# RWKV attention and cosine router: splitting dense TensorE stages around single groups of transposes

## Chip, cores and metric

The kernel runs on one core of a Trainium2 chip. The metric is the device time of one execution in microseconds (us), the median over runs. TensorE is PE (its weight loads PEld), VectorE DVE, ScalarE ACT, GpSimd POOL, and SyncE, which issues most DMAs, SP.

## What is computed

A linear attention over 768 steps for 4 batches and 8 heads of dimension 48 gives 3072 rows of 384. A router picks one of 8 experts for each row by cosine similarity, and that expert's two layers (384 to 1024 to 384) give the row of the output.

```python
for t in range(S):
    cur = einsum('bhd,bhe->bhde', u * k[t], v[t])
    y[:, :, t] = einsum('bhd,bhde->bhe', r[t], state + cur)
    state = w * state + einsum('bhd,bhe->bhde', k[t], v[t])
x = rows of y, heads side by side                     # 3072 x 384
logits = normalised(x) @ normalised(expert_emb).T / tau
e = argmax(logits); gate = softmax(logits)[e]
out = gate * (relu(x @ w1[e]) @ w2[e])
```

## The kernel before

The attention works in 12 turns (TURNS). Turn t takes chunk t // 2 of 128 steps for two of the four batches; u = 0, 1 numbers these two. Within a turn the chunk falls into two halves of 64 steps (s), and the 8 heads into four pairs (p) of two (par), each head padded to 64 partitions.

What a turn does for the inputs of step t, by function and line:

- `scale_r`, `scale_k` (L377, L373, POOL) multiply R and K by powers of the decay, giving Rw and Kw, a turn ahead.
- `turn_in` (L393, PE) transposes Rw or Kw of one u: four 128x128 transposes into one bank. For u=0 the banks are ps0 (Rw) and ps1 (Kw), for u=1 ps2 and ps3. `take_in` (L409 for Rw, L407 for Kw, ACT) copies the bank to RT or KT, and `own_r` (L420, DVE) writes the second half of RT from the same bank, times u.
- `scores` (L433, PE) multiplies KT and RT of one u into ps0 and ps1 (u=0) or ps2 and ps3 (u=1), in 48x64 tiles, four at a time. `mask` (L448) and `own_terms` (L455), both DVE, read these banks into AT.
- `outer` (L469, PE) multiplies Kw and V into the banks pu0 (first half of the chunk) and pu1 (second half), in 64x64 tiles, for both u. `half_state` (L485; L483 in the first chunk) adds pu0 to the state, `next_state` (L490) adds pu1, both DVE; `decay_state` (L496, POOL) follows.

And a turn later, for its output:

- `with_v` (L524, PE, two phases) and `with_state` (L543, PE, one part for each s) accumulate y in the banks py0 and py1; `between` (L512, ACT) peeks at the banks between the phases; `take_y` (L550, ACT, twice) copies them to YT.
- `turn_y` (L558, PE) transposes YT of u=0 into pu0 and of u=1 into pu1, four transposes each; `take_x` (L562, ACT) copies a bank to X, `keep_x` (L587, SP) stores X in DRAM, `squares` (L593, ACT) sums its squares.
- The router's steps for a chunk (`logits` L600, `take_logits` L608, `choose_a` L639 on POOL, `choose`, `scale` L665, `ranks` L686, `rows_of` L844, `put` L867 and others) are spread over the following turns.

The order on every engine is written by hand. `attention` gives each call a planned time (`plan.at`), turns being PERIOD = 9.4 apart, and `Plan.emit` issues the calls sorted by these times. Each engine runs its instructions in the order in which they were issued; semaphores wait for data and for banks to come free. A number in `plan.at` therefore sets only a place in the queues. `after` makes loads and early weight loads wait for the last PE instruction issued before them.

Before the change, the place of the transposes is set by

```python
plan.at(before + 3.3 + 2.35 * u + 0.47 * place, turn_in, k, t, u, which)
plan.at(at + 4.75, outer, k, t)
plan.at(at + 5.6, half_state, k, t)
plan.at(nxt + a[5] + 0.45 * u, turn_y, k, t, u)
```

so that, in a middle turn, PE does: scores (both u), router matmuls, with_v, with_state (both s), Rw and Kw of u=0, with_v, outer (both u), Rw and Kw of u=1, output of u=0 and of u=1, and in every other turn logits. After turn 11 come the experts (`first_layer` L1165, `group` L1243, `layer2` L1383 and others), which the change doesn't touch.

Of the kernel before, what the change touches and what calls it, by code (L numbers as in the profile page):

```python
# [70 lines left out]
def halves(s):  # L71
    return slice(s * HC, (s + 1) * HC)
# [272 lines left out]
def of(ring, t):  # L345
    return ring[t % len(ring)]
# [111 lines left out]
    )  # L458


def outer(k, t):
    Kw, V = of(k.Kw, t), of(k.V, t)
    last = t // 2 == NCH - 1
    for u in range(2):
        for p in range(NP):
            for s in range(1 if last else 2):
                for par in range(2):
                    h, col = 2 * p + par, (u * NP + p) * D
                    k.last = k.nc.tensor.matmul(  # L469
                        k.U[s][par * DP : (par + 1) * DP, col : col + D],  # L470
                        Kw[halves(s), u, h, :], V[halves(s), u, h, 0:D],
                        start=True, stop=True, skip_group_check=True,
                    )
# [407 lines left out]
def attention(k):  # L881

    plan = Plan()
    P = PERIOD
    end = (TURNS - 1) * P
    for t in range(TURNS):
        at = t * P
        c, bp = divmod(t, 2)
        before, nxt = at - P, at + P
        for i in range(6 if t else 0):  # L890
            when = at - 3 * P + 0.5 + 1.55 * i
            if t < 4:

                if t < 3 and i > 3:
                    continue
                plan.at(when, load, k, t, i // 2 if t > 2 else i % 2, i % 2 if t > 2 else i // 2, slice(0, H), False)
                if t < 3 and i == 3:
                    for v in ((0,), (1, 2))[t - 1]:
                        for w in range(2):
                            plan.at(when + 0.1 * v + 0.01, load, k, v, 2, w, slice(0, H), False)  # L900
                continue
            for j in range(2):
                plan.at(when + 0.75 * j, load, k, t, i // 2, i % 2, slice(j * NP, (j + 1) * NP))
        for u in range(2):
            for which in range(2):

                place = which if t else 1 - which
                if t:
                    plan.at(before + 1.0 + 2 * u + place, scale_k if which else scale_r, k, t, u)
                plan.at(before + 3.3 + 2.35 * u + 0.47 * place, turn_in, k, t, u, which)  # L910
                plan.at(before + 3.8 + 2.4 * u + 0.6 * place, take_in, k, t, u, which)
            plan.at(before + (4.0 if t else 4.75) + 2.6 * u, own_r, k, t, u)
            plan.at(at + 0.9 * u, scores, k, t, u)
            for par in range(2):
                plan.at(at + 0.9 + 1.5 * u + 0.36 * par, mask, k, t, u, par)
                plan.at(at + 1.65 + 1.5 * u + 0.4 * par, own_terms, k, t, u, par)
        if t < TURNS - 1:
            plan.at(at + 4.75, outer, k, t)
            plan.at(at + 5.6, half_state, k, t)
        else:  # L920
            plan.at(at + 5.0, outer, k, t)
            plan.at(at + 5.3, half_state, k, t)
        if c < NCH - 1:
            plan.at(at + 6.2, next_state, k, t)
            plan.at(at + 6.8, decay_state, k, t)
        if t < TURNS - 2:
            a = (1.8, 2.3, 3.3, 4.25, 5.0, 6.65, 7.4, 8.4)
            plan.at(nxt + a[0], with_v, k, t, 0)
            plan.at(nxt + a[1], with_state, k, t)
            plan.at(nxt + a[2], between, k, t)  # L930
            plan.at(nxt + a[3], with_v, k, t, 1)
            for par in range(2):
                plan.at(nxt + a[4] + 0.6 * par, take_y, k, t, par)
            for u in range(2):
                plan.at(nxt + a[5] + 0.45 * u, turn_y, k, t, u)
                plan.at(nxt + a[6] + 0.5 * u, take_x, k, t, u)
                plan.at(nxt + a[6] + 0.1 + 0.5 * u, keep_x, k, t, u)
                plan.at(nxt + a[7] + 0.7 * u, squares, k, t, u)
        else:

            for when, fn, *args in (
                (
                    (3.0, with_v, 0), (3.5, with_state), (4.6, between), (5.6, with_v, 1),
                    (5.65, take_y, 0), (5.7, take_y, 1), (7.6, turn_y, 0), (7.75, take_x, 0), (7.9, turn_y, 1),
                    (7.76, keep_x, 0), (8.5, take_x, 1), (8.51, keep_x, 1), (9.5, squares, 0), (9.55, squares, 1),
                ),
                (
                    (6.8, with_v, 0), (6.82, with_state, (0,)), (7.5, with_state, (1,)), (7.7, between),
                    (7.8, with_v, 1), (8.2, take_y, 0), (8.4, take_y, 1), (10.0, turn_y, 0), (10.02, turn_y, 1),
                    (10.4, take_x, 0), (10.41, keep_x, 0), (10.5, take_x, 1), (10.51, keep_x, 1),  # L950
                    (10.7, squares, 0), (10.75, squares, 1),
                ),
            )[t - TURNS + 2]:
                plan.at(end + when, fn, k, t, *args)
        if bp == 1 and c < NCH - 1:
            plan.at(nxt + 7.6, logits, k, c)
            plan.at(nxt + 8.6, take_logits, k, c)
            then = nxt + P
            plan.at(then + 1.78, turn_logits, k, c)
            if c < NCH - 2:  # L960
                plan.at(then + 2.42, keep_logits, k, c)
                plan.at(then + 6.9, choose_a, k, c)
                plan.at(then + 7.5, choose, k, c)
                plan.at(then + 8.9, scale, k, c)
                plan.at(then + 9.0, exps, k, c)
                then += P
                plan.at(then + 1.79, ranks, k, c)
                plan.at(then + 2.42, placed, k, c)
                plan.at(then + 7.5, places, k, c)
                plan.at(then + 8.7, gate, k, c)  # L970
                plan.at(then + 8.8, values, k, c)
                plan.at(then + 8.9, rows_of, k, c)
                plan.at(then + P + 3.25, put, k, c)
                plan.at(then + P + 3.95, collect, k, c)
            if c == SETTLE[0]:
                plan.at(then + 2.43, count, k, c)
                plan.at(then + 5.0, settle, k, c)
                plan.at(then + 5.05, settled, k)

    c = NCH - 2  # L980
    for t, fn, *args in (
        (1.0, choose_a, k, c),
        (3.96, first_lists, k, 0),
        (4.0, keep_logits, k, c),
        (4.2, choose, k, c),
        (5.5, scale, k, c),
        (6.3, exps, k, c),
        (6.85, ranks, k, c),
        (6.9, placed, k, c),
        (6.95, count, k, c),  # L990
        (7.3, places, k, c),
        (7.4, settle, k, c),
        (7.45, sort_embeddings, k),
        (7.5, sort_counts, k),
        (8.4, gate, k, c),
        (8.8, values, k, c),
        (8.9, rows_of, k, c),
        (11.2, put, k, c),
        (11.25, collect, k, c),
        (11.3, first_lists, k, 1),  # L1000
        (11.35, settled, k),
    ):
        plan.at(end + t, fn, *args)
# [3 lines left out]
    c = NCH - 1  # L1007
# [790 lines left out]
def kernel(  # L1798
# [43 lines left out]
    with tc.manual_schedule(), ExitStack() as long_ctx:  # L1842
        n.long = long_ctx.enter_context(tc.tile_pool(name="long", bufs=1))
        with ExitStack() as attention_ctx:
            n.aconst = attention_ctx.enter_context(tc.tile_pool(name="aconst", bufs=1))
            rings(n)
            build_first(n)
            n.rt = attention_ctx.enter_context(tc.tile_pool(name="rt", bufs=2))
            attention(n)
        with ExitStack() as experts_ctx:  # L1850
            n.gp1 = experts_ctx.enter_context(tc.tile_pool(name="gp1", bufs=1))
            n.gp = experts_ctx.enter_context(tc.tile_pool(name="gp", bufs=4))
            experts(n)
# [29 lines left out]
```

## Time and profile before

| | |
|---|---|
| Median of 3 runs | 391.32 us (389.54 to 393.18) |
| The profiled execution | 415.55 us, span 413.7 us |
| Mean granted TensorE clock | 0.964 |
| PE busy | 383.0 us, 93% of the span |
| PEld busy | 349.9 us, 85% |
| DVE busy | 236.4 us, 57% |
| ACT busy | 138.2 us, 33% |
| POOL busy | 189.2 us, 46% |
| Chain of waits that ended last | PE 76%, issue 9% |

The attention fills about 8 to 121 us of the span. In the profile, a row of the timeline is start and length in us, engine, line, operation, what is written and read, shapes and number of records; in brackets stands idle time of the engine just before, with what ended it. A matmul of 32-bit floats leaves two records, a transpose one. Lengths of PE rows include the pipeline's latency, so neighbouring rows overlap; starts are measured. In the chain of waits, "issue" is time in which the engine waited for nothing that the profile shows.

### The profile page before, as it was taken

How to read it: one execution, taken by the hardware profiler on the slowest of the kernel's cores; microseconds unless marked ns; L12 is line 12 of the kernel's file. 1: busy time of each engine (PE TensorE's matmuls, PEld its weight loads, DVE VectorE, ACT ScalarE, POOL GpSimd, SP SyncE). 2: the span in 40 equal slices, each digit the busy share in tenths (PEclk: the TensorE clock that was granted, in tenths of full speed). 3: DMA queues.
4: the chain of work that ended last, by engine and by line, in shares of the span. 5: the costliest groups of instructions: out<-in, count | busy, mean ns of one | idle time of the engine just before them, and what ended most of it. 6: DMA issues, size and time to landing. Idle time of an engine off the chain costs nothing.

```text
span 413.7 us, 12753 instructions
## 1 busy us (share of the span) xinstructions
PE 383.0 (93%) x5055; PEld 349.9 (85%) x5055; DVE 236.4 (57%) x603; ACT 138.2 (33%) x357; POOL 189.2 (46%) x222
## 2 busy tenths in 40 slices
PE   8889899999989996999989997699999999999993
PEld 5778788888878895989779997699999989989982
DVE  7957787878885650532843744155546546465331
ACT  4464546465524521221023212221321321422410
POOL 3875656555530354420377427501753855702002
PEclk9999999999996996899999999689999999999998
DMA  9988788788154573263953553144454446101001
GB/s 157 198 165 174 158 172 181 146 183 179 44 178 142 162 238 104 73 164 93 315 178 90 126 182 93 42 111 136 132 137 142 144 133 199 62 10 57 0 2 65
DMA packets 100232, 54.44 MB, mean 132 GB/s; under 512 B 80897, under 2 KB 95275, under 8 KB 100162
## 3 DMA queue, kind: packets, MB, share of 16 engines
q1 hardware_dynamic: 93218, 43.68, 41.6%
q0 software_dynamic: 4448, 9.45, 7.5%
q8 instruction: 42, 0.69, 0.7%
q10 hardware_dynamic: 2496, 0.40, 0.5%
q14 instruction: 28, 0.23, 0.2%
HBM read 44.25 MB, written 9.58 MB: 130 GB/s over the span
## 4 chain that ended last, share of the span: by engine, by line
PE 76%; issue 9%; DVE 2%; another core or an unknown queue 2%; POOL 1%; ACT 1%; POOLq 0%; DVEq 0%; ACTq 0%
PE ps L1243 9%; PE ps L1383 8%; PE ps L1165 7%; PE ps L1364 6%; PE pu L1243 5%; PE ps L433 4%; PE ps L393 4%; PE pu L1383 4%; PE py L1243 4%; PE py L1383 3%; PE pu L558 3%; PE py L524 3%; PE py L1165 3%; PE py L543 2%; PE pu L469 2%
## 5 line engine op out<-in xcount | busy, mean ns | idle before, releaser
L1123 POOL DMA_INDIRECT G<-xs,quarters x76 | 83.7, 1101 | 50.5 <-issue 38.8
L1342 POOL DMA_INDIRECT out_dram<-y,goes x27 | 28.3, 1048 | 97.0 <-DVE y L1352 41.3
L1165 PE MATMUL ps<-RT,w 128*128 128x128 f32 x204 | 30.1, 299 | 4.4 <-ACT R L1168 1.9
L1165 PEld LDWEIGHTS ps<-RT,w 128*128 128x128 f32 x204 | 27.3, 210 | 5.9 <-issue 2.3
L377 POOL TENSOR_TENSOR Rw<-R,rpow 128x384 f32<-128x384 f32 x22 | 22.8, 1037 | 14.2 <-PE ps L433 8.0
L1243 PE MATMUL ps<-xTe,w 128*128 128x192 f32 (+3 forms) x132 | 27.0, 339 | 0.0
L433 PE MATMUL ps<-RT,KT 48*64 48x128 f32 x768 | 25.3, 275 | 0.2
L433 PEld LDWEIGHTS ps<-RT,KT 48*64 48x64 f32 x768 | 21.1, 132 | 3.7 <-issue 2.5
L373 POOL TENSOR_TENSOR Kw<-K,kpow 128x384 f32<-128x384 f32 x22 | 23.8, 1081 | 0.5 <-DMA R<-in_r_dram 0.5
L1243 PEld LDWEIGHTS ps<-xTe,w 128*128 128x128 f32 x132 | 23.4, 194 | 0.1
L496 POOL TENSOR_TENSOR T<-T,wC 128x384 f32<-128x384 f32 x10 | 8.3, 827 | 27.1 <-DVE T L490 27.1
L448 DVE TENSOR_TENSOR AT<-ps,smask 128x256 f32<-128x256 f32 x48 | 18.6, 414 | 1.2 <-PE ps L433 1.2
L409 ACT COPY RT<-ps 128x512 f32<-128x512 f32 x22 | 12.9, 585 | 18.3 <-PE ps L393 16.9
L455 DVE COPY_PREDICATED AT<-dmask,ps 128x256 f32<-128x256 int32 x48 | 18.5, 441 | 0.0
L1270 ACT ACTIVATE RT<-RT 128x384 f32<-128x384 f32 (+1 forms) x18 | 9.5, 532 | 26.1 <-DVE RT L1182 18.6
L1243 PE MATMUL ps<-Tx,S 128*128 128x192 f32 (+3 forms) x76 | 16.5, 348 | 1.2 <-issue 1.1
L420 DVE TENSOR_TENSOR RT<-ps,uw 128x512 f32<-128x512 f32 x22 | 15.2, 690 | 4.2 <-ACT RT L409 3.9
L393 PE MATMUL ps<-ident,Rw 128*128 128x128 f32 x96 | 15.4, 283 | 2.2 <-DVE AT L455 1.0
L1383 PE MATMUL ps<-T,RT 128*128 128x192 f32 x96 | 17.3, 327 | 0.0
L1270 ACT ACTIVATE hT<-hT 128x432 f32<-128x432 f32 (+2 forms) x18 | 9.7, 541 | 21.2 <-DVE hT L1182 16.1
L1383 PEld LDWEIGHTS ps<-T,RT 128*128 128x128 f32 x96 | 15.9, 190 | 0.9
L469 PE MATMUL pu<-V,Kw 64*64 64x48 f32 x704 | 14.4, 218 | 2.4 <-issue 2.3
(380 smaller groups left out, 917.0 us busy)
## 6 DMA issues: line engine op xcount, KB each, us to landing
w<-in_moe_w_dram SPq DMA_DIRECT2D x96, 128.0 KB
w<-in_moe_w_dram SPq DMA_DIRECT2D x24, 384.0 KB
xs<-X SPq DMA_DIRECT2D x24, 192.0 KB
K<-in_k_dram SPq DMA_DIRECT2D x32, 96.0 KB
R<-in_r_dram SPq DMA_DIRECT2D x32, 96.0 KB
V<-in_v_dram SPq DMA_DIRECT2D x32, 96.0 KB
w<-in_moe_w_dram SPq DMA_DIRECT2D x16, 192.0 KB
V<-in_v_dram SPq DMA_DIRECT2D x8, 192.0 KB
```

Of the source, the lines that this page charges most:

```text
L373: q.tensor_mul(of(k.Kw, t)[:, u, :, 0:D], of(k.K, t)[:, u] if t else raw(k, 0)[:, u, :, 0:D], k.kpow)
L377: ins = k.nc.gpsimd.tensor_mul(of(k.Rw, t)[:, u, :, 0:D], of(k.R, t)[:, u], k.rpow)
L393: k.last = k.nc.tensor.transpose(bank[:, p * C : (p + 1) * C], pair(src[:, u], p), k.ident)
L433: ins = k.nc.tensor.matmul(k.D[2 * u + par][halves(s), p * C : (p + 1) * C], KT[rows, u, p, halves(s)], RT[rows, u, p, s].rearrange("q j i ...
L469: k.last = k.nc.tensor.matmul(k.U[s][par * DP : (par + 1) * DP, col : col + D], Kw[halves(s), u, h, :], V[halves(s), u, h, 0:D], start=Tru ...
L1123: k.nc.gpsimd.indirect_dma_start(out=k.GG[e % 2][:, g * QUARTER : (g + 1) * QUARTER], out_offset=None, in_=k.xs.rearrange("n (q c) -> (n q ...
L1165: k.last = k.nc.tensor.matmul(ps, w1[:, m, f * 128 : (f + 1) * 128], x_of(k, e, m)[:, cols], start=(m == 0), stop=(m == NK - 1))
L1243: k.last = nc.tensor.matmul(ps[:, i * h : (i + 1) * h], a[:, g, i * 128 : (i + 1) * 128], b, start=start and i == 0, stop=True, skip_group ...
L1270: nc.scalar.activation(out(i, c), out(i, c), ACT.Relu)
L1342: k.nc.gpsimd.indirect_dma_start(out=out[:, :], out_offset=IndirectOffsetOnAxis(ap=k.goes[0:n, e, t : t + 1], axis=0), in_=y[0:n, :], in_o ...
L1364: k.last = k.nc.tensor.matmul(k.two[e][m], a, b, start=(f == 0), stop=(f == NF - 1))
L1383: k.last = nc.tensor.matmul(ps, a(q), b[:, q], start=start and q == 0, stop=True, skip_group_check=True,)
```

## The change

Four kinds of calls get other planned times; no computation is added or removed.

- `outer` takes its u as an argument and is planned twice, so that `turn_in` of Rw for u=1 can stand between its two parts, and Kw for u=1 after the second. `half_state` moves from at + 5.6 to at + 6.16, just behind `own_r` of u=1, which moves from before + 6.6 to before + 6.15.
- `with_state` is planned for s=0 and s=1 apart, with Rw of u=0 between them and Kw of u=0 after them. In the first chunk, where with_state has no part s=0, Rw of u=0 stands ahead of it.
- `turn_y`, `take_x`, `keep_x` and `squares` of u=1 move to the next turn, where `turn_y` stands between scores of u=0 and of u=1.
- `choose_a` for chunk NCH - 2 moves from 1.0 to 2.3 within the last turn.

```diff
-def outer(k, t):
+def outer(k, t, us=(0, 1)):
...
-    for u in range(2):
+    for u in us:
...
-                plan.at(before + 3.3 + 2.35 * u + 0.47 * place, turn_in, k, t, u, which)
-                plan.at(before + 3.8 + 2.4 * u + 0.6 * place, take_in, k, t, u, which)
-            plan.at(before + (4.0 if t else 4.75) + 2.6 * u, own_r, k, t, u)
+                if t:
+                    plan.at(before + ((2.75, 3.8), (5.3, 6.35))[u][place], turn_in, k, t, u, which)
+                    plan.at(before + ((3.4, 4.4), (6.1, 6.8))[u][place], take_in, k, t, u, which)
+                else:
+                    plan.at(before + 3.3 + 2.35 * u + 0.47 * place, turn_in, k, t, u, which)
+                    plan.at(before + 3.8 + 2.4 * u + 0.6 * place, take_in, k, t, u, which)
+            plan.at(before + ((4.0, 6.15) if t else (4.75, 7.35))[u], own_r, k, t, u)
...
-            plan.at(at + 4.75, outer, k, t)
-            plan.at(at + 5.6, half_state, k, t)
+            for u in range(2):
+                plan.at(at + 4.75 + u, outer, k, t, (u,))
+            plan.at(at + 6.16, half_state, k, t)
...
-            a = (1.8, 2.3, 3.3, 4.25, 5.0, 6.65, 7.4, 8.4)
+            a = (1.8, 2.3, 3.75, 4.25, 5.0, 6.65, 7.4, 8.4)
             plan.at(nxt + a[0], with_v, k, t, 0)
-            plan.at(nxt + a[1], with_state, k, t)
+            for s in range(2):
+                plan.at(nxt + a[1] + s, with_state, k, t, (s,))
             plan.at(nxt + a[2], between, k, t)
             plan.at(nxt + a[3], with_v, k, t, 1)
...
             for u in range(2):
-                plan.at(nxt + a[5] + 0.45 * u, turn_y, k, t, u)
-                plan.at(nxt + a[6] + 0.5 * u, take_x, k, t, u)
-                plan.at(nxt + a[6] + 0.1 + 0.5 * u, keep_x, k, t, u)
-                plan.at(nxt + a[7] + 0.7 * u, squares, k, t, u)
+                over = u * (P + 0.5 - a[5])
+                plan.at(nxt + a[5] + over, turn_y, k, t, u)
+                plan.at(nxt + a[6] + over, take_x, k, t, u)
+                plan.at(nxt + a[6] + 0.1 + over, keep_x, k, t, u)
+                plan.at(nxt + a[7] + over, squares, k, t, u)
...
-        (1.0, choose_a, k, c),
+        (2.3, choose_a, k, c),
```

## The prediction, made before the changed kernel ran

> **What bounds the kernel now.** I read the stages first: busy time, granted clock and DMA share of the attention (16 to 121 us of the span) and of the rest.
>
> ```profile
> 16.00:121.00 105.00, 98.71 (x3098) 87.77 (x3092) 81.59 (x246) 55.80 (x153) 61.47 (x89) 1.00 0.73 157
> 121.00:414.00 293.00, 271.07 (x1783) 252.86 (x1778) 141.27 (x326) 75.24 (x188) 119.71 (x111) 0.95 0.40 120
> ```
>
> The columns are stretch, length, PE, PEld, DVE, ACT, POOL, clock, DMA share, GB/s. In the attention PE is busy 98.71 of 105 us at full clock (1.00). The chain of waits, read next, agrees: from 30 to 122 us it stays on PE almost throughout, and its other pieces are "issue", two of which are
>
> ```profile
> 72.35 0.95 issue
> 90.02 0.43 issue
> ```
>
> With the others in the attention (0.74 at 20.3, 1.00 at 42.0, 1.08 at 50.7, 0.40 at 68.8, 0.51 at 102.5) they come to 5.1 us. They fall inside runs of equal matmuls, where no semaphore is due. So a turn is a queue of PE stages back to back, and whatever lengthens that queue lengthens the kernel. Then one turn of PE in the timeline (start, length):
>
> ```profile
> 78.31 0.69 PE L524 MATMUL py<-AT,V 64*64 64x64 f32 x32
> 78.83 0.63 PE L543 MATMUL py<-RT,T 48*48 48x64 f32 x32
> 79.28 0.63 PE L543 MATMUL py<-RT,Tmid 48*48 48x64 f32 x32
> 79.83 1.10 PE L867 MATMUL pu<-QV,P 128*128 128x64 f32 x8
> 80.77 0.61 PE L393 MATMUL ps<-ident,Rw 128*128 128x128 f32 x4
> 81.22 0.60 PE L393 MATMUL ps<-ident,Kw 128*128 128x128 f32 x4
> 81.75 0.69 PE L524 MATMUL py<-AT,V 64*64 64x64 f32 x32
> 82.26 1.10 PE L469 MATMUL pu<-V,Kw 64*64 64x48 f32 x64
> 83.29 0.66 PE L393 MATMUL ps<-ident,Rw 128*128 128x128 f32 x4
> 83.78 0.60 PE L393 MATMUL ps<-ident,Kw 128*128 128x128 f32 x4
> 84.22 1.10 PE L558 MATMUL pu<-ident,YT 128*128 128x128 f32 x8
> 85.25 1.98 PE L433 MATMUL ps<-RT,KT 48*64 48x128 f32 x64
> ```
>
> Lengths overlap, so I use start to start. Four transposes between transposes take 0.44 (83.78 to 84.22). As the first after a tiled stage they take 0.49 (83.29 to 83.78), and as the last before one 0.53 (81.22 to 81.75). Thirty-two 64-column records take 0.45 after a tiled stage (78.83 to 79.28), 0.52 after transposes (81.75 to 82.26), 0.55 before a full-array stage (79.28 to 79.83). Entering the full array from tiles costs (0.55-0.45)+(0.49-0.44)=0.15 us, leaving it (0.53-0.44)+(0.52-0.45)=0.16. **One interruption of a tiled stage by transposes costs 0.31 us beside the transposes themselves.**
>
> Last, ACT and DVE at the end of that turn:
>
> ```profile
> 82.51 1.07 ACT L550 COPY YT<-py 128x512 f32<-128x512 f32 x2
> 83.40 0.56 DVE L485 TENSOR_TENSOR Tmid<-T,pu 128x384 f32<-128x384 f32 x1 [0.67 <-PE pu L469]
> 83.98 0.58 ACT L409 COPY RT<-ps 128x512 f32<-128x512 f32 x1 [0.40 <-PE ps L393]
> 84.06 0.56 DVE L490 TENSOR_TENSOR T<-Tmid,pu 128x384 f32<-128x384 f32 x1
> 84.60 0.69 DVE L420 TENSOR_TENSOR RT<-ps,uw 128x512 f32<-128x512 f32 x1
> ```
>
> half_state (L485) runs first and frees bank pu0 before the output's transposes need it; own_r (L420) comes last and starts 0.04 after ACT's L409 ends (84.56). The list of waits has the same pair, in whose order lies the trouble below:
>
> ```profile
> DVE RT L420 <- ACT RT L409: 3.9, 6, 1.1
> ```
>
> **What the Trainium skill says.** "TensorEngine Tiling", Key Properties: changing the tiling mode drains TensorE. The trace agrees: 0.15 in, 0.16 out. "TensorE: Matmul & The Clock Gate", Part 1: the clock halves after a window of some 3.4 us with too little PE activity; Part 4: transposes don't count as activity in the same way. Here the clock stays at 1.00 although every turn has a run of 16 transposes (83.29 to 85.25 is one), so the trace gives that no support. "Runtime: NRT & Kernel Launch", Instruction fetch mechanics: instructions arrive in blocks of 256 by the engine's own DMA queue. The page's 42 packets and 0.69 MB on one instruction queue fit PE's 10110 records, and I read the "issue" pieces as late blocks.
>
> **The change, part by part.** No work is added or removed. R and K stand for the transposes of Rw and Kw, Y for those of the output, 0 and 1 for the half u.
>
> 1. *Interruptions.* R1 goes inside outer (turns 0 to 10: 11), R0 inside or ahead of with_state (turns 1 to 10: 10; where L867 follows R0 it shares the full array), Y1 inside scores (turns 2 to 11: 10). In each case the order of PE before had these beside other transposes. 31 x 0.31 = +9.6 us. The seam between Y0 and Y1 (a wait, some 0.05) goes: 10 x 0.05 = -0.5.
>
> 2. *Y0 now waits for half_state.* The changed program's DVE order has own_r of u=1 ahead of half_state and next_state in every turn; before, it was behind. Let S be the start of outer (82.26). PE: half of outer 0.47, in 0.10, R1 0.49, out 0.09, other half 0.47+0.07, in 0.10, K1 0.49: Y0 could start at S+2.28. DVE: ACT ends its two L550 copies at S+1.32, whatever R1 does; L409 for R1 queues behind them, to S+1.90; own_r S+1.94 to 2.63; half_state to S+3.15; with the 0.05 seen between L490's end (84.62) and Y1, Y0 starts at S+3.2. Stall 0.92, against none before (S+1.96), in turns 1 to 9. In turn 10 other DVE work already delays half_state, and I count 0.4. Sum +8.7. Late next are scores, which stand behind Y0, and through decay_state and choose_a the router's work on DVE.
>
> 3. *R0 may wait for the masks of u=0.* It moves 0.45 nearer to scores, while masks queue on DVE behind routing (P, L844, takes 1.49 at 77.69). Following the row from S, bank 0 comes free about 0.2 after PE is ready in turns with P and 0.1 in those with choose: 9 turns, +1.0 (bounds 0 and 3).
>
> 4. *Off the path.* ten take_x and squares of u=1 come a turn later on ACT, which sits idle 3.03 us before L512 at 79.95; if that cover went, 1.1 us each would delay R0's copy, not PE. Their ten stores on SP move behind two K loads and hold the K, R and V loads queued after them; these feed scaling a turn ahead, so 0; without the slack up to 1 us a turn. choose_a in turn 11 has POOL's 3.41 idle us before L1113: 0. POOL's scaling starts when scores of u=0 end, which Y1's move advances: 0.
>
> 5. *Given back.* A turn gains about 1.8 us and holds about 580 PE records with weight loads, 2.3 blocks, so each block gets 0.8 us more to arrive. Taking 0.8 off each late block (1.00 to 0.2, 1.08 to 0.3, 0.95 to 0.15, the others to 0) gives -4.4 (bounds -5.1 and 0: a run without the profiler may have no such holes).
>
> Sum: 9.6-0.5+8.7+1.0-4.4 = +14.4 us. The profiled execution took 415.55 (span 413.7), so its like would take 430. The runs have a median of 391.32, 24 below, but their attention does the same PE work, so I add the same: **405.7**.
>
> Bounds: an interruption 0.15 (half hidden) to 0.35, 4.7 to 10.9; the stall 0 to 1.2 each; with the others +5 to about +24.
>
> **Rivals.**
> - *Drains only* (0.17): own_r does not hold up half_state, say because L409 overtakes. For: turns with much DVE work show it idle. Against: L420 follows L409 each time. 9.1+1.0, less 2.5 given back: +7.6, 399.
> - *The clock falls too* (0.15): the end of a turn would have the stall and 0.75 us of drains in some 4 us. For: after three "issue" holes between 122.2 and 124.4 the clock averages 0.67 over 121 to 131. Against: single 1 us holes at 42 and 51 did not do it. Four half-rate windows of 3.4 us lose 1.7 each: +7, 412.
> - *Instruction supply is the bound* (0.05): waits then vanish under it, 391. The profile gives 5.1 us over some 25 blocks, 0.2 each; it decides from 0.8.
> - *Not slower: the clock gains* (0.08): in unprofiled runs clusters of transposes might halve the clock, and separating them prevent it. Each window saved is worth 1.7; from 9 windows it outweighs 14.4; ten give 388.7. Against: not one between 16 and 121 us.
>
> **How the numbers follow.** The forecast has 0.55, with 400 to 410 as its own range. About 1% is what a measurement of this kernel can tell from no change (its runs spread from 389.54 to 393.18). Faster by over 1% is most of the last rival, 0.06; within 1% supply and its rest, 0.06; slower 0.88. The range 397 to 413 takes in drains only and most of the falling clock.
>
> **What would show it.** In the new profile: 469, 433 and 543 split, each split with 0.3 us beyond its transposes (right if 25 to 40 such); Y0 (L558, first four) idle about 0.9 before it, released by DVE's half_state (wrong if Y0 follows K1 within 0.2); "issue" in the attention below 2 us; the stages from turn 11 on unchanged but later by 14 us; the clock at 1.00 up to there. A clock below 1 in the attention, or turns of unchanged length, would make it wrong.

## The result and the profile after

The changed kernel takes 401.44 us (median of 6 runs, 400.06 to 404.63), the kernel before beside it 391.23 us (6 runs, 389.54 to 393.18). The ratio is 1.0264, with an interval of 1.0225 to 1.0303: slower by about 10.2 us, where 14.4 were forecast. Ratios, here and below, leave out the runs that took over 1.5% longer than the fastest of their kernel.

The two profiled executions can't be set against each other as wholes: the one of before (span 413.7 us) has stretches of half clock after the attention, the one of after (span 399.1) has none before its last microseconds. The attention is free of that in both, so I measure it alone, from the first scores (L433) of turn 0 to the first scores of turn 11. The starts in the traces are 8.81 and 115.69 us before, 10.25 and 127.32 after: **106.9 and 117.1 us, a difference of 10.2 us, the same as the timed one.** In this pair the loss is all in the attention.

The attention as one stretch of the kernel after (stretch, length, PE, PEld, DVE, ACT, POOL, clock, DMA share, GB/s):

```profile
16.00:127.50 111.50, 101.63 (x2925) 83.22 (x2929) 81.90 (x231) 58.16 (x149) 59.98 (x87) 1.00 0.66 140
```

The clock stays at 1.00 throughout the attention, as before; PE is idle for 10 us of it instead of 6. What it waits for is told by the list of waits of PE in the attention (us in total, times, longest), which in the kernel before is "issue" for 5.1 us, R0 for the masks (L455) once for 1.0, and three other pieces of 0.4 and less:

```profile
PE ps L393 <- issue: 2.4, 3, 1.0
PE pu L469 <- issue: 2.3, 3, 1.1
PE ps L393 <- DVE AT L455: 1.0, 1, 1.0
PE py L543 <- issue: 0.4, 1, 0.4
```

Of the kernel after:

```profile
PE pu L558 <- ACT KT L407: 3.8, 5, 0.8
PE ps L393 <- DVE AT L455: 1.9, 3, 0.8
PE pu L558 <- DVE Tmid L485: 1.3, 2, 0.8
PE ps L393 <- POOL Rw L377: 1.1, 2, 0.8
PE pu L558 <- DVE over L828: 0.8, 1, 0.8
PE pu L469 <- issue: 0.4, 1, 0.4
```

"issue" has fallen to 0.4 us: the late instruction blocks are gone. That "issue" on PE is a late block shows in a count of PE's matmul and weight load records in order of start: each of the seven pieces in the attention of the kernel before has 193 or 194 records of its block of 256 ahead of it, and so has every piece in the attention of the other traces. In their place stand the wait ahead of Y0 (L558), 5.9 us in eight pieces, and a longer wait ahead of R0 (L393), 3.0 us for banks (L455) and Rw (L377). The end of a turn in the timeline of after shows the first of them:

```profile
91.33 0.66 PE L393 MATMUL ps<-ident,Kw 128*128 128x128 f32 x4
91.44 0.69 DVE L420 TENSOR_TENSOR RT<-ps,uw 128x512 f32<-128x512 f32 x1 [2.57 <-ACT RT L409]
92.02 0.58 ACT L407 COPY KT<-ps 128x512 f32<-128x512 f32 x1 [0.61 <-PE ps L393]
92.05 0.54 DVE L485 TENSOR_TENSOR Tmid<-T,pu 128x384 f32<-128x384 f32 x1
92.74 0.63 PE L558 MATMUL pu<-ident,YT 128*128 128x128 f32 x4 [0.76 <-ACT KT L407]
```

K1 is done, and DVE, after 2.57 us of waiting for ACT's copy of R1 (L409), does own_r (L420, 91.44) and only then half_state (L485, 92.05 to 92.59), and Y0 starts at 92.74. The profile names ACT's L407 as the releaser: it ends at 92.60, within 0.01 us of half_state. Two engines that end together can't be told apart from such a row; the first experiment does it.

**A sum over gaps.** For every run I took the start-to-start gaps of successive PE records in the attention and divided its length in two: "waits", what a clearly long gap (by some 0.1 us or more) exceeds the ordinary pitch, and "rest". Before: 10.3 + 96.6. After: 13.2 + 103.9. So waits grew by 2.9 us and the rest, where the drains of split stages must lie, by 7.3. The line between the two isn't sharp: a long gap at a change of tiling holds a drain too, and the limit for "long" moves some 1 us from one part to the other.

### The profile page after: what moved, and what is told of

Its sections match the earlier page's. It is cut to its first block, busy times and chain, and to the rows that moved or that the text cites. A ratio compares the mean times of both kernels' runs of the same rounds, so it can differ in the third digit from the quotient of the medians.

```text
span 399.1 us, 12727 instructions
## 1 busy us (share of the span) xinstructions
PE 378.0 (95%) x5055; PEld 339.2 (85%) x5055; DVE 239.7 (60%) x603; ACT 142.4 (36%) x357; POOL 189.1 (47%) x222
## 4 chain that ended last, share of the span: by engine, by line
PE 74%; issue 9%; DVE 6%; POOL 4%; DMA 2%; ACT 2%; POOLq 0%; SPq 0%; DVEq 0%; ACTq 0%
PE ps L1252 10%; PE ps L1392 8%; PE ps L1373 6%; PE ps L1174 6%; PE pu L1252 5%; PE ps L393 5%; PE py L1252 4%; PE pu L1392 4%; PE py L1392 3%; PE ps L433 3%; PE py L524 3%; PE pu L558 2%; PE py L1174 2%; PE py L543 2%; DMA R<-in_r_dram 2%
## 5 line engine op out<-in xcount | busy, mean ns | idle before, releaser
L420 DVE TENSOR_TENSOR RT<-ps,uw 128x512 f32<-128x512 f32 x22 | 15.2, 689 | 21.5 <-ACT RT L409 21.5
L377 POOL TENSOR_TENSOR Rw<-R,rpow 128x384 f32<-128x384 f32 x22 | 22.8, 1036 | 11.1 <-ACT rpow L143 6.4
L1174 PE MATMUL ps<-RT,w 128*128 128x128 f32 x204 | 26.2, 278 | 1.4 <-ACT R L1177 0.6
L433 PE MATMUL ps<-RT,KT 48*64 48x128 f32 x768 | 27.1, 277 | 0.2
L1174 PEld LDWEIGHTS ps<-RT,w 128*128 128x128 f32 x204 | 24.2, 192 | 2.0 <-ACT R L1177 0.8
L433 PEld LDWEIGHTS ps<-RT,KT 48*64 48x64 f32 x768 | 20.8, 133 | 5.0 <-issue 4.0
L558 PE MATMUL pu<-ident,YT 128*128 128x128 f32 x96 | 15.3, 283 | 6.1 <-ACT KT L407 3.8
L448 DVE TENSOR_TENSOR AT<-ps,smask 128x256 f32<-128x256 f32 x48 | 18.5, 413 | 1.0 <-PE ps L433 0.9
L409 ACT COPY RT<-ps 128x512 f32<-128x512 f32 x22 | 12.9, 586 | 17.1 <-PE ps L393 14.8
L558 PEld LDWEIGHTS pu<-ident,YT 128*128 128x128 f32 x96 | 10.1, 141 | 10.1 <-ACT KT L407 6.8
L393 PE MATMUL ps<-ident,Rw 128*128 128x128 f32 x96 | 15.5, 284 | 3.4 <-DVE AT L455 1.9
L455 DVE COPY_PREDICATED AT<-dmask,ps 128x256 f32<-128x256 int32 x48 | 18.5, 438 | 0.0
L407 ACT COPY KT<-ps 128x512 f32<-128x512 f32 x22 | 12.9, 586 | 11.2 <-PE ps L393 10.8
```

Of the source, the lines that this page charges most:

```text
L377: ins = k.nc.gpsimd.tensor_mul(of(k.Rw, t)[:, u, :, 0:D], of(k.R, t)[:, u], k.rpow)
L393: k.last = k.nc.tensor.transpose(bank[:, p * C : (p + 1) * C], pair(src[:, u], p), k.ident)
L433: ins = k.nc.tensor.matmul(k.D[2 * u + par][halves(s), p * C : (p + 1) * C], KT[rows, u, p, halves(s)], RT[rows, u, p, s].rearrange("q j i ...
L558: k.last = k.nc.tensor.transpose(k.rows[u][:, g * C : (g + 1) * C], YT[:, u, g % 2, g // 2, :], k.ident)
L1174: k.last = k.nc.tensor.matmul(ps, w1[:, m, f * 128 : (f + 1) * 128], x_of(k, e, m)[:, cols], start=(m == 0), stop=(m == NK - 1))
```

## The experiments

The last pair (one row again, before again) ran beside a before that takes 391.15 us, the others beside ones of 416.86 (the first four) and 414.21 (the next four), where runs spread over 10 us and more. What is slower there lies behind the attention: the kernel after takes 427.65 us there and has the same attention to 0.1 us. Its clock from 130 to 400 us is 0.97 instead of 0.99, which is some 5 of the 26 us; the rest of them stays open. So ratios from there are wide, and the attention's length is the better measure. The expectations in absolute times took a before of 391 us for granted; of them only the differences count.

| kernel | attention | waits | rest | ratio to before beside it | of the medians of all runs |
|---|---|---|---|---|---|
| before | 106.9 | 10.3 | 96.6 | 1 | 1 |
| before, again | 106.2 | 9.9 | 96.3 | 1.0042 [1.0012, 1.0071] | 1.001 |
| after | 117.1 | 13.2 | 103.9 | 1.0264 [1.0225, 1.0303] | 1.026 |
| after, again | 117.1 | 13.4 | 103.7 | 1.0495 [1.0377, 1.0613] | 1.032 |
| outer split only | 112.4 | 12.0 | 100.4 | 0.997 [0.9864, 1.0075] | 1.013 |
| Y1 in scores only | 107.5 | 9.1 | 98.4 | 1.0134 [1.0046, 1.0222] | 1.004 |
| R0 in with_state only | 109.8 | 11.2 | 98.6 | 1.0172 [1.0108, 1.0237] | 1.007 |
| order on DVE only | 119.8 | 23.2 | 96.6 | 1.0439 [1.03, 1.0578] | 1.034 |
| after, own_r behind | 115.2 | 11.5 | 103.7 | none | 1.024 |
| after, own_r behind, R0 and K0 back | 111.0 | 9.4 | 101.7 | 1.0207 [1.0019, 1.0394] | 1.010 |
| one row of transposes | 111.6 | 15.0 | 96.6 | 1.0253 [1.0133, 1.0373] | 1.009 |
| one row, again | 111.0 | 15.4 | 95.6 | 1.0073 [1.0043, 1.0103] | 1.010 |

The kernel before against itself gives 1.0042, so a ratio that near to 1 says nothing, whatever its interval. Several ratios disagree with their profiles: 5.5 us more of attention are 1.3%, above the interval of the outer's split; 0.7 and 3.0 us are 0.2% and 0.7%, below those of Y1 and R0, and one row and after again lie above what their lengths come to as well. These ratios rest on few runs (the outer's split on 2 of its 22, against 8 of 27 of before). The medians of all runs come within 0.4% of what the lengths give, but for after again (1.032, where 10.2 us are 2.5%), and that stays unexplained. So the argument below rests on the lengths.

### after, own_r behind half_state

```diff
-plan.at(before + ((4.0, 6.15) if t else (4.75, 7.35))[u], own_r, k, t, u)
+plan.at(before + ((4.0, 6.6) if t else (4.75, 7.35))[u], own_r, k, t, u)
```

Theory H: half_state behind own_r is what Y0 waits for. Rival L: ACT's copy of K1, as the profile says.

> The changed kernel with one place altered: own_r of u=1 stands behind half_state and next_state on DVE again. Theory H (Y0 waits for half_state, which own_r delays): the idle time before the output's transposes, 6.1 us in the attention of the changed kernel, falls to about 1 us; some 1 us of late instruction blocks comes back; 396 us, between 394.5 and 398. Rival L (Y0 waits for ACT's copy L407, which the list of waits names for 3.8 of the 6.1 us): the DVE order doesn't matter, 400 to 402. Rival D (31 interruptions of 0.31 us are the whole loss): 400 to 402.

In the timeline of this kernel, at the end of the same turn:

```profile
89.47 0.66 PE L393 MATMUL ps<-ident,Kw 128*128 128x128 f32 x4
89.57 0.55 DVE L485 TENSOR_TENSOR Tmid<-T,pu 128x384 f32<-128x384 f32 x1 [2.56 <-PE pu L469]
90.16 0.59 ACT L407 COPY KT<-ps 128x512 f32<-128x512 f32 x1 [0.61 <-PE ps L393]
90.27 0.63 PE L558 MATMUL pu<-ident,YT 128*128 128x128 f32 x4
90.70 0.68 DVE L420 TENSOR_TENSOR RT<-ps,uw 128x512 f32<-128x512 f32 x1
```

Y0 starts at 90.27, when L407 has only begun (it ends at 90.75), and 0.15 after half_state's end: L is refuted, H stands. But the attention shortened by 1.9 us, not by the 5 that the wait was worth. Its list of PE waits says where the rest went:

```profile
PE ps L393 <- DVE AT L455: 5.9, 6, 1.1
...
PE pu L558 <- DVE Tmid L485: 0.3, 2, 0.2
```

Y0's wait fell from 5.9 to 0.5 (with 0.2 for L483), but R0's rose from 3.0 to 6.2 (0.3 of it for Rw). The size of H's forecast was wrong: it took the stall off PE without asking who is next. DVE was just behind, as the timeline shows earlier in the same turn:

```profile
84.04 0.77 DVE L455 COPY_PREDICATED AT<-dmask,ps 128x256 f32<-128x256 int32 x2
...
84.61 0.63 PE L393 MATMUL ps<-ident,Rw 128*128 128x128 f32 x4 [1.04 <-DVE AT L455]
```

In such a turn DVE has the router's L858 (1.19 us from 80.85) and L844 (1.49 from 81.96) ahead of the masks L448 (from 83.37) and L455, and runs without a break up to the mask that frees R0's bank; a PE that comes earlier waits there.

### Each split alone

The three, each in the kernel before:

```diff
-plan.at(at + 4.75, outer, k, t)
-plan.at(at + 5.6, half_state, k, t)
+for u in range(2):
+    plan.at(at + 4.75 + u, outer, k, t, (u,))      # R1 at before + 5.3
+plan.at(at + 5.9, half_state, k, t)
```

> Before, with only outer split around R1 (own_r behind, as before). Theory H: 11 interruptions x 0.31 = 3.4 us, and since half_state now ends with the second half of outer just as Y0 is due, up to 0.25 us a turn for Y0 and Y1, 2.5 more; 1.5 given back by late blocks: 395.5, between 394 and 397. Rival L: 3.4 less 1, 393.5. Rival D: 3.4, 394.6.

```diff
+over = u * (P + 0.5 - a[5])
-plan.at(nxt + a[5] + 0.45 * u, turn_y, k, t, u)
+plan.at(nxt + a[5] + over, turn_y, k, t, u)        # take_x, keep_x, squares likewise; choose_a as in the change
```

> Before, with only the output's transposes of u=1 moved between the scores of the next turn. Theories H and L: 10 x (0.31 - 0.05) = 2.6 us, 0.6 given back: 393.2, between 392 and 394.5. Rival D: the same without giving back, 393.8. If ACT's later copies or the stores on SP mattered: 395 or more.

```diff
-plan.at(nxt + a[1], with_state, k, t)
+for s in range(2):
+    plan.at(nxt + a[1] + s, with_state, k, t, (s,))  # R0 at before + 2.75, K0 at + 3.8; between at + 3.75
```

> Before, with only with_state split around R0. Theories H and L: 10 x 0.31 = 3.1 us, plus waits of R0 for the masks on DVE or for POOL of 1 to 2 us, 1 given back: 394.8, between 393 and 396. Rival D: 394.3 and no idle time before R0.

In the rest of the sum, where drains are, the outer's split costs 100.4 - 96.6 = 3.8 us, Y1's 1.9, R0's 2.0. Together 7.7, against 7.3 for all three in the kernel after: the costs add up. Divided by the number of splits they are not the price of one, because the rest also takes in short waits and leaves out drains that stand in a long gap. That price is read at the seams, start to start, where nothing is awaited. Y1 in scores only:

```profile
85.82 0.60 PE L558 MATMUL pu<-ident,YT 128*128 128x128 f32 x4
86.35 1.10 PE L433 MATMUL ps<-RT,KT 48*64 48x128 f32 x32
87.38 0.66 PE L558 MATMUL pu<-ident,YT 128*128 128x128 f32 x4
87.97 1.10 PE L433 MATMUL ps<-RT,KT 48*64 48x128 f32 x32
89.01 0.41 PE L686 MATMUL pu<-cum_oh,umask 128*128 128x32 f32 x2
```

From Y0 to the router's L686 these are 3.19 us, where the kernel before takes 2.94 (84.22 to 87.16): 0.25 more. Before has a wait of 0.06 between Y0 and Y1 there (the two take 1.03, and 0.97 where nothing is awaited) that is gone, so the interruption is 0.31. R0 in with_state, in the kernel after in a turn where R0 waits for nothing, and below it the same of the kernel before:

```profile
39.92 0.63 PE L543 MATMUL py<-RT,T 48*48 48x64 f32 x32
40.48 0.66 PE L393 MATMUL ps<-ident,Rw 128*128 128x128 f32 x4
41.07 0.66 PE L543 MATMUL py<-RT,Tmid 48*48 48x64 f32 x32
41.66 0.66 PE L393 MATMUL ps<-ident,Kw 128*128 128x128 f32 x4
42.25 0.69 PE L524 MATMUL py<-AT,V 64*64 64x64 f32 x32
...
47.41 0.63 PE L543 MATMUL py<-RT,T 48*48 48x64 f32 x32
...
49.44 0.69 PE L524 MATMUL py<-AT,V 64*64 64x64 f32 x32
```

2.33 us against 2.03: 0.30 for the interruption (and 0.25 where L867 shares the full array: 3.17 from 62.67 us on, against 2.92 from 78.83 before). In the outer's split, first part, R1 and second part take 1.76 us (100.02 to 101.78 after; outer and R1 1.52 before), and K1 behind a tiled stage 0.49 (78.85 to 79.34 in the outer's own kernel) instead of 0.44: 0.29. So the three stages cost nearly the same. The whole lengths (+5.5, +0.7, +3.0, where +4.3, +2 and +3.6 were expected) differ from these by the waits, whose sum is +1.7, -1.2 and +0.9 against before's. In the outer's split late blocks of 4.8 us remain, and half_state, which needs both parts of outer, now ends behind K1, so that Y0 starts 0.42 after K1's last transpose. R0's split has, on its own, the wait for the masks:

```profile
PE ps L393 <- DVE AT L455: 4.5, 7, 1.0
...
PE ps L393 <- POOL Rw L377: 0.7, 1, 0.7
```

5.2 us for banks and Rw, 3.9 more than before's 1.3, where the prediction had 1.0 for this step: without Y0's stall the move costs much more than with it (3.0 in the kernel after). That is what the first experiment ran into.

### The order on DVE alone

The kernel before with nothing changed on PE:

```diff
-plan.at(at + 5.6, half_state, k, t)
+plan.at(at + 6.61, half_state, k, t)
-plan.at(at + 6.2, next_state, k, t)
+plan.at(at + 6.62, next_state, k, t)
```

> The kernel before with nothing split and nothing moved on TensorE: only half_state and next_state are put behind own_r of the second half on VectorE, as in the kernel after. Compared by the attention's length (first scores of turn 0 to first scores of turn 11, 106.9 us in the kernel before) and by the ratio to the kernel before. Theory D (the order on VectorE makes Y0 wait): here K1's transposes follow R1's at once, so the chain eviction of R1's half by ScalarE 0.58, own_r 0.69, half_state 0.54 stands bare ahead of Y0: about 1.6 to 1.8 us for each of 10 turns, 16 to 18, of which up to 5 us of late instruction blocks come back: +11 to +13, ratio 1.028 to 1.034. Theory S (only the splits cost, the order on VectorE is nothing): 0, ratio 1.00.

The attention is 12.9 us longer (11 to 13 were expected; the ratio of 1.0439 lies above the 1.034 of that text, with 1.03 as its lower end): theory D holds, and its sum too. In the timeline:

```profile
102.45 0.60 PE L393 MATMUL ps<-ident,Kw 128*128 128x128 f32 x4
...
103.27 0.69 DVE L420 TENSOR_TENSOR RT<-ps,uw 128x512 f32<-128x512 f32 x1 [1.59 <-ACT RT L409]
103.88 0.55 DVE L485 TENSOR_TENSOR Tmid<-T,pu 128x384 f32<-128x384 f32 x1
...
104.57 1.15 PE L558 MATMUL pu<-ident,YT 128*128 128x128 f32 x8 [1.52 <-DVE Tmid L485]
```

K1, then 1.52 us of nothing on PE: copy, own_r, half_state, one after the other. The chain is the one that the prediction had, only bare, because no second half of outer stands between R1 and K1. Its rest is 96.6, as before's: nothing was split. (Of its waits, 1.8 us are matmuls stretched by half clock, told of at the end.) The list of waits gives the price and what came back for it:

```profile
PE pu L558 <- DVE Tmid L485: 12.1, 8, 1.5
...
PE ps L433 <- issue: 0.3, 1, 0.3
PE pu L469 <- issue: 0.2, 1, 0.2
```

With 1.5 each ahead of Y0 for L483 and L828 it is 15.1 us of stall, and late blocks of 0.5 instead of 5.1. So the blocks come in time when PE waits: this kernel has no drains beyond before's, and the late blocks are gone as they are in after. Drains alone didn't do that: with the outer's split 4.8 us of late blocks remain, with Y1's 4.9.

### after, own_r behind, and R0 and K0 back

```diff
-plan.at(before + ((2.75, 3.8), (5.3, 6.35))[u][place], turn_in, k, t, u, which)
+plan.at(before + ((3.3, 3.77), (5.3, 6.35))[u][place], turn_in, k, t, u, which)
-for s in range(2):
-    plan.at(nxt + a[1] + s, with_state, k, t, (s,))
+plan.at(nxt + a[1], with_state, k, t)
```

with own_r of u=1 at before + 6.6, as in the first experiment.

> The kernel after with two things undone: own_r of the second half stands behind half_state and next_state, and R0 and K0 come one after the other behind an undivided with_state. Left are the outer's split (11) and Y1 between the scores' halves (10). Theory W (what removing the Y0 stall freed in the run with own_r behind went into R0's wait for the masks, 5.9 us there): with R0 later that wait has cover, so 10 splits fewer (3.1) and about 3 to 5 us of waits less: attention 4 to 6 us longer than before's 106.9, ratio 1.010 to 1.016. Theory P (every stall removed comes back in the next place, wherever it is): attention stays about 115, 8 us longer, ratio 1.020 or more.

The attention is 111.0 us, 4.1 longer than before's: theory W. R0's wait for the masks is down from 5.9 to 1.0, Y0's is 0.4, and late blocks are back, 3.4 us of them:

```profile
PE pu L469 <- issue: 2.4, 3, 1.3
PE ps L393 <- DVE AT L455: 1.0, 1, 1.0
```

Waits are at 9.4, below before's 10.3; what is left of the loss is the rest, +5.1: the drains of outer and scores (3.8 and 1.9 alone).

### One row of transposes a turn

The change turned round:

```diff
-plan.at(at + 4.75, outer, k, t)
-plan.at(at + 5.6, half_state, k, t)
+plan.at(at + 3.35, outer, k, t)
+plan.at(at + 4.3, half_state, k, t)                 # next_state at + 4.9
-plan.at(before + 3.3 + 2.35 * u + 0.47 * place, turn_in, k, t, u, which)
+plan.at(before + 5.2 + 0.9 * u + 0.45 * place, turn_in, k, t, u, which)   # t > 0; copies, own_r and L867 with it
```

> The opposite of the change: in the kernel before the outer product moves ahead to stand right behind with_state, and all six groups of transposes of a turn (R0 K0 R1 K1 Y0 Y1) stand in one row behind the second with_v, so TensorE goes from the tiled stages to whole-array transposes and back once a turn instead of twice. half_state and next_state move ahead with the outer product. Theory D+S: 10 interruptions fewer at 0.31 us are -3.1; own_r and half_state are far from each other; late instruction blocks may take back up to 1: attention 104 to 105, ratio 0.992 to 0.996. Rival: four evictions in a row by ScalarE (0.58 each against 0.31 for a group of transposes) make the scores or Y0 wait for their buffers, 0.3 to 0.5 us a turn: nothing gained or +2, ratio 1.000 to 1.005.

> The kernel with one row of transposes a turn once more. In its first run the clock stood at 0.91 in two stretches of 20 us of the attention, and instruction blocks came late for about 7 us. If the clock was the chip's and not the order's, it is 1.00 in the attention here, and the attention is 3 to 4 us shorter than the 111.6 us of the first run, 107.5 to 109, still not shorter than before's 106.9, because the late blocks remain. If the order itself (16 to 24 transposes in a row, and the tiled stages in one stretch) brings the clock down, it is 0.91 again and the length 111 to 112.

> The kernel before beside it on the same chip: attention 106.9 us at clock 1.00, with some 5 us of late instruction blocks, ratio 1.00. If this chip's clock falls in the attention whatever the order, the clock is below 1.00 there in this run too.

This was meant to beat both and doesn't: 111.6 us of attention, and 111.0 when run again, where the kernel before has 106.2 and 1.00 of clock between 20 and 60 us. Neither of my forecasts held, the rival's of +2 included. (A group of four transposes takes 0.44 us, as the prediction has it, not 0.31.) The list of waits of the second run:

```profile
PE pu L469 <- issue: 3.5, 3, 2.4
PE pu L469 <- DVE lg L627: 3.3, 3, 1.1
PE py L524 <- issue: 2.0, 2, 1.7
```

With 0.8 ahead of L393 there are 6.3 us of late blocks, where before beside it has 4.7: with_v, with_state, outer and scores now follow one another without the pause of transposes. Outer, moved ahead, waits 3.3 us for a bank that the router's logits hold until DVE copies them (L627), and 1.5 us are waits for own_r (L420), the kind that the rival had named. And the clock fell: from 22.3 us on, in the stretches' view (same columns as above),

```profile
18.00:22.30 4.30, 1.93 (x119) 1.80 (x112) 1.91 (x6) 0.22 (x2) 4.22 (x17) 1.00 0.94 182
...
24.00:25.00 1.00, 1.00 (x6) 1.00 (x7) 0.11 (x1) 1.00 (x3) 0.81 (x1) 0.50 1.11 215
...
26.00:27.00 1.00, 1.00 (x11) 1.00 (x10) 0.31 (x1) 1.00 (x3) 0.00 (x0) 1.00 0.49 86
```

PE was busy for 1.93 of 4.30 us, behind a late block of 2.4 us, and then ran at half clock for some 3.4 us (0.58 over 22.3 to 24, 0.50 to 26), which costs about 1.7. The rest is 95.6 with this in it, so about 93.9 without: 2.4 below the 96.3 of before beside it, near the 3.1 forecast for ten drains fewer. By this count the drains were saved; a bank, late blocks, own_r and the clock took more than that.

## Why the prediction was right in direction and too high

By its own steps, in us over the attention (start to start, from the gaps of the two traces):

| step | forecast | measured |
|---|---|---|
| 1. interruptions | 9.1 | 7.3 (8.8 at the seams) |
| 2. Y0's stall | 8.7 | 7.4 |
| 3. R0's wait | 1.0 | 1.9 |
| 4. ACT, SP, POOL | 0 | 0 |
| 5. late blocks | -4.4 | -5.3 |
| other waits of before, absorbed | not in the sum | -1.1 |
| sum | 14.4 | 10.2 |

**The mechanisms held**, and those of the largest two terms are shown by experiments: drains (three kernels with one split each), and the order of own_r and half_state (the order alone, and its undoing).

**Step 1** holds at the seams: 0.29 to 0.31 us for an interruption, 0.25 in three places where L867 shares the full array. The 31 come to 9.1, and 0.3 of waits between Y0 and Y1 went (0.5 forecast): 8.8. The rest column shows only 7.3, because a drain in a long gap counts there as a wait. If 8.8 is taken, the waits grew by 1.4 and not by 2.9, and the rows of the waits below it are together 1.5 too high; which of them wasn't separated.

**Step 2** had the right chain, and the stall of 0.92 came to within 0.02 (Y0 starts 1.03 to 1.05 after K1's last transpose, 0.11 of it pitch) in 7 of the 10 turns; in the others a late block or another wait stood ahead in the same turn, and 0.7, 0.2 and 0.2 were left. I charged each turn as if nothing else could be late in it, and took 0.4 for turn 10, which has the whole stall.

**Step 3** was low: 1.0 was forecast, 1.9 measured, within the bounds. The experiments show that it is tied to step 2: in PE's list of waits R0's is 1.3 us before, 3.0 after, and without Y0's stall 5.2 (R0's split alone) to 6.2 (own_r behind). The prediction added the two as if they were independent.

**Step 4** held: no wait in the list of after ends on a load, on take_x or squares. Only POOL's scaling, put there at 0, ends two of R0's waits (1.1 us, 0.3 before); I count them in step 3.

**Step 5** was right to 0.9 us, and the order alone shows that waits of PE are enough for it. That drains help too, as the step assumed with its 1.8 us a turn, isn't shown. What I left out is its like: other short waits of before, which a slower turn absorbs too.

**The rivals.** "Drains only" falls with the order-alone kernel. "The clock falls too" and "the clock gains" fall with a clock of 1.00 in the attention of both kernels; in the changed kernel no part of the difference is left for them. That the timed difference is the profiled one leaves no sign of a gain without the profiler either. "Instruction supply is the bound" would have needed more than the 5 us that it gave back.

The Trainium skill, "TensorEngine Tiling", Key Properties, says that a change of tiling mode drains TensorE; the runs agree, with 0.25 to 0.31 us for a stage split once. "TensorE: Matmul & The Clock Gate", Part 1, gives a window of about 3.4 us for the clock; the half clock behind the idle stretch of the one-row kernel lasted that long, 3.4 us (22.58 to 26.00).

## What to carry to other kernels

When instructions of an in-order engine are moved, look at what now stands ahead of the step that frees a bank: one eviction moved 0.45 ahead in the plan made TensorE wait 0.9 us a turn, and the order alone costs more (12.9 us) than the whole change. Price a split of a tiled stage by its seam, start to start, where nothing is awaited: about 0.3 us here, for three different stages. Before a stall is counted as gain, find the engine that ends next: of 5.4 us taken off Y0, 3.2 came back at R0, until R0 stood later too.

## What was not expected of the hardware

**Late instruction blocks depend on waits.** In kernels of nearly the same PE work, "issue" on PE in the attention is 5.1 us (before), 0.4 (after), 0.5 (order alone, with 15.1 us of stall), 4.8 and 4.9 (more drains, but few waits), 2.9 (R0's split alone, with 5.2 of waits), and 6.3 where the tiled stages follow one another without transposes in between.

**The clock halves behind idle TensorE, but not each time, and only at steps of 3.41 us.** In every trace the changes of the granted clock lie whole multiples of 3.413 us apart: in the kernel before, half clock begins at 124.32 us and ends two steps later (131.15), and begins again after eight more (158.45), for three (168.69). In the order-alone kernel it fell once in the attention, right behind 1.5 us of idle ahead of Y0, and not behind other stalls of that length. Laid on its steps, the stretch ahead of the fall, the one of half clock, and one with such a stall and no fall:

```profile
33.05:36.46 3.41, 1.88 (x19) 1.45 (x17) 2.00 (x6) 1.07 (x2) 0.03 (x1) 1.00 0.85 220
36.46:39.87 3.41, 3.41 (x49) 2.60 (x52) 1.56 (x7) 2.09 (x6) 1.51 (x3) 0.50 0.94 179
...
101.31:104.73 3.42, 1.90 (x61) 1.64 (x53) 1.80 (x4) 2.01 (x4) 0.00 (x0) 1.00 0.81 156
```

Where a gap lies against the steps matters. In one row's first run a late block that ends at 54.5 us stands within one step (51.22 to 54.63, PE busy for 1.45 us), and the clock fell; when run again, a block that ends at 54.5 us is cut by a step's end at 53.30 (2.96 and 2.18 us busy), and it didn't. The four falls in the attentions follow steps with 1.00, 1.45, 1.56 and 1.88 us of busy PE; no step there that kept the clock has less than 1.89. That is no threshold yet: 1.88 and 1.89 are too near for rows with modelled ends, and behind the attention the clock fell after 2.13 us (before, 120.91 to 124.32) and held after 1.58 (own_r behind, R0 and K0 back, 257.26 to 260.67). What is weighed within a step stays open. Transposes do count in it, against what the prediction cites of them: in the order-alone kernel the step from 56.94 to 60.35 has nothing on PE but 16 transposes, 1.89 us of busy PE, and the clock stays at 1.00, which in no trace it does after a step with less than 1.58.
